# Where the output-projection steps stand in the opening half of a tile pair: behind each column part's down steps, or behind those of all parts

## The chip, the cores and the metric

The kernel runs on one core of one Trainium2 chip. Its engines here are PE (TensorE, the matrix engine; PEld are its weight loads), DVE (VectorE), ACT (ScalarE) and SP (SyncE, which issues DMAs). The metric is the device time of one execution in microseconds (us), the median of several runs.

## The reference

For 2048 tokens of width 640, the program computes a linear attention (32 heads of 20) and a feed-forward block (inner width 1728), and mixes them with a gate per token:

```
g = sigmoid((x * gate_w).sum(-1, keepdims=True))
a = attention(x) @ wo                                   # o: 2048 x 640, wo: 640 x 640
b = (gelu(x @ w_gate) * (x @ w_up)) @ w_down            # w_down: 1728 x 640
return g * a + (1 - g) * b
```

The two final products go to the same output. The kernel folds the gate ratio into the attention output, adds both products up in the same PSUM bank (a piece of the memory that matmuls write to), and scales once at the eviction.

## The kernel before

The change lies in the last stage. Tokens stand in 16 tiles of 128, taken in pairs; four tiles are a block. For each pair the output's 640 columns are cut into parts (320 + 320; in the last pair 256 + 256 + 128). For each part, the opening half of a pair takes 14 "down" steps (hidden chunk times `w_down`) and 5 "output-projection" steps (`goT`, the transposed and gated attention output, times `wo`). A step is two matmuls side by side, one on rows 0 to 63 of the array, one on rows 64 to 127. In the opening half of a pair, row half r works for tile r; in the closing half they swap, so that each tile gets both halves of the contraction.

```python
        # in down_pair(t0, banks, widths), a generator; mm() issues one matmul
        def mm(r, j, h, c, opens, x, n):          # row half r, tile j, part h, chunk c, step x of n
            ...
            w, end = widths[h], x == n - 1
            ...
            sc.op("pe", lambda e: e.matmul(self.bank(bk, w), lhs, rhs, start=opens and x == 0, stop=end and not opens,
                                           skip_group_check=True),
                  reads=rd, writes=[("ps", bk)] + ([("turn", bk)] if end else []), signal=end,
                  after=[("turn", bk)] if x == 0 and not opens else ())
        ...
        for q in range(2 * nw):
            h, opens = q % nw, q < nw
            cs = list(range(NFC + 1 if opens else NFC)) + [NFC + 1 + k for k in range(KD)]
            for x, c in enumerate(cs):
                for r in (0, 1):
                    mm(r, r if opens else 1 - r, h, c, opens, x, len(cs))
                if x == len(cs) - 1 and not opens:
                    evac(h)
                yield None
```

The closing half has 13 down steps, since the fourteenth chunk has only 64 rows and is done in one go. `after=[("turn", bk)]` is the wait at the swap: the first closing matmul into a bank waits until the other row half's last opening matmul into it has been written.

Between steps, the attention numerator of a later tile is computed (`num`): 20 short matmuls, a chain of VectorE operations that ends in the tile `Og`, and a DMA that transposes `Og` into `goT`. Positions are counted in steps of a block:

```python
        def downs(b, side):
            ...
                    n += 1
                    if n in side:
                        self.num(side[n])
        ...
        at = (1, 31, 61, 91)
        ...
        for b in range(self.NB):
            downs(b, {at[k]: 4 * b + 2 + k for k in range(4 if b < 3 else 2)})
```

In a block the second `num` makes `goT` for the fourth tile, which the second pair needs.

The softmax here doesn't subtract the row's maximum and nothing guards it: scores larger than these inputs give would overflow.

Of the kernel before, what the change touches and what calls it, by code (L numbers as in the profile page):

```python
# [107 lines left out]
class _Kernel:  # L108
    S, D, H, DH, F = 2048, 640, 32, 20, 1728
    KD = D // P  # L110
# [4 lines left out]
    NFC = 14  # L115
# [576 lines left out]
    def down_pair(self, t0, banks, widths):  # L692

        sc = self.sc
        ts = (t0, t0 + 1)
        NFC, KD = self.NFC - 1, self.KD
        nw = len(widths)
        hk = t0 // 4
        last = t0 + 2 == self.NT
        os_ = t0 % 4  # L700

        def mm(r, j, h, c, opens, x, n):
            t = ts[j]
            tt, gs, bk, w0, a = t % 4, t % 8, banks[h][j], sum(widths[:h]), 64 * r
            w, end = widths[h], x == n - 1
            if c <= NFC:
                lhs, rhs = self.hT(hk, c)[a:a + 64, tt * P:(tt + 1) * P], self.wd_sb[a:a + 64, c, w0:w0 + w]
                rd = [("hT", hk, c), "wd"] if c < NFC else [("hT", hk, 13, r), ("wd13", r)]
            else:
                k = c - NFC - 1  # L710
                lhs, rhs = self.goT[a:a + 64, gs, k, :], self.wo_sb[a:a + 64, k, w0:w0 + w]
                rd = [("goT", gs), "wo"]
# [5 lines that stand above are left out]
        def evac(h):  # L718
            w0, w = sum(widths[:h]), widths[h]
            for j in (0, 1):  # L720
                bk, dst, g = banks[h][j], self.outsb[:, os_ + j, w0:w0 + w], self.Gm[:, ts[j]:ts[j] + 1]
                rd, wr = [("ps", bk), "Gm"], [("outsb", os_ + j, h)]
                if last and j == 1:
                    sc.op("dve", lambda e: e.tensor_scalar(dst, self.bank(bk, w), g, None, op0=ALU.mult), reads=rd, writes=wr)
                else:
                    sc.op("act", lambda e: e.activation(dst, self.bank(bk, w), AF.Copy, scale=g), reads=rd, writes=wr)  # L726
            if last:
                hs, c0, c1 = [h], w0, w0 + w
            elif h == nw - 1:
                hs, c0, c1 = range(nw), 0, self.D  # L730
            else:
                return
            if t0 < self.TB:
                rows = self.out[0:self.BT, :].rearrange("(p j) n -> p j n", j=self.TB)[:, t0:t0 + 2, :]
            else:
                rows = self.out[t0 * P:(t0 + 2) * P, :].rearrange("(j p) n -> p j n", p=P)
            sc.dma("sp", lambda e: e.dma_start(rows[:, :, c0:c1], self.outsb[:, os_:os_ + 2, c0:c1]),
                   reads=[("outsb", os_ + j, k) for j in (0, 1) for k in hs], writes=[("out", t0, h)])

        for q in range(2 * nw):  # L740
            h, opens = q % nw, q < nw
            cs = list(range(NFC + 1 if opens else NFC)) + [NFC + 1 + k for k in range(KD)]
            for x, c in enumerate(cs):
                for r in (0, 1):
                    mm(r, r if opens else 1 - r, h, c, opens, x, len(cs))
                if x == len(cs) - 1 and not opens:
                    evac(h)
                yield None

# [94 lines left out]
```

## Time and profile before

| | before |
|---|---|
| time, median of 3 runs (range) | 288.31 us (287.94 to 288.32) |
| span of the profiled run | 287.0 us |
| last stage, from its first down matmul to the start of the last ScalarE eviction | 197.89 to 284.12 = 86.23 us |
| one step of 320 columns in it | 0.136 us |

The first view is the page: busy time of each engine, then two of the costliest groups. A group's columns are: source line, engine, operation, what is written and read, shape, count, then busy us and mean ns of one, then the engine's idle time just before.

```profile
PE 280.9 (98%) x3017; PEld 185.7 (65%) x3032; DVE 174.9 (61%) x353; ACT 104.5 (36%) x199; POOL 5.3 (2%) x36
...
L713 PE MATMUL ps<-wd_sb,hT 64*128 64x320 bf16 x648 | 49.4, 296 | 0.0
...
L713 PE MATMUL ps<-wo_sb,goT 64*128 64x320 bf16 (+2 forms) x340 | 27.8, 288 | 0.0
```

PE, the matrix engine, is busy 98% of the span. The 340 output-projection matmuls (those that read `goT`) and the 648 down matmuls shown had 0.0 us of idle time before them. They never waited for anything. The page's share of the chain that ended last says the same of the whole kernel:

```profile
PE 96%; DMA 2%; issue 1%; SPq 0%; ACT 0%
```

The chain in order of time (start us, length us, engine and line) shows the stage itself. L713 is the down and output-projection matmul, L657 the `num` matmul, L354 the matmuls of the stage before.

```profile
196.93 1.03 PE ps L354 x4
197.96 0.24 PE ps L713 x2
198.20 0.39 PE ps L657 x20
198.59 4.08 PE ps L713 x60
202.67 0.39 PE ps L657 x20
203.06 4.07 PE ps L713 x60
207.13 0.39 PE ps L657 x20
...
211.99 7.88 PE ps L713 x116
...
284.12 0.37 ACT outsb L726
```

The chain never leaves PE until the last eviction. A run of 60 matmuls is 30 steps in 4.07 to 4.08 us, 0.136 us each, and each `num` takes 0.39 us. The Trainium skill ("TensorE: Matmul & The Clock Gate", section Back-to-back issue gap) gives N/2.4 + 2.5 ns as the isolated warm gap, 135.8 ns for N = 320: this trace agrees. The stage is a sum of matmul times with nothing between them.

The timeline of ScalarE (start us, length us, operation, idle time before it and its end) gives the time at which banks come free; the first line is the end of the last pair but one, the second the end of the kernel's matmul work.

```profile
273.98 0.94 ACT L726 ACTIVATE outsb<-ps,Gm 128x320 bf16<-128x320 f32 x2 [1.50 <-PE ps L713]
...
284.12 0.37 ACT L726 ACTIVATE outsb<-ps,Gm 128x128 bf16<-128x128 f32 x1 [0.53 <-PE ps L713]
```

The two evictions of a part take 0.94 us together.

### The profile page before, as it was taken

Reading aid. Unit: us, or ns where it says so; the run is one execution under the profiler, and the core shown is the slowest. Engines: PE = TensorE matmul, PEld = TensorE weight load, DVE = VectorE, ACT = ScalarE, POOL = GpSimd, SP = SyncE. Lnnn points to the kernel's source line nnn. Section 1 sums busy time; section 2 is a strip of 40 time slices with the busy share of each in tenths; the row PEclk is TensorE's granted clock in tenths of the full one; section 3 lists DMA queues with packets and bytes.
Section 4 is the critical chain, followed back from the end, with each engine's and each line's share of the span. In section 5 each row is a group of like instructions: output and inputs, shape, how many; then the busy total and the mean of one; then the engine's idle time right before and its main releaser. Section 6 shows DMA issues by size and latency. Waiting matters only on the chain.

```text
span 287.0 us, 7005 instructions
## 1 busy us (share of the span) xinstructions
PE 280.9 (98%) x3017; PEld 185.7 (65%) x3032; DVE 174.9 (61%) x353; ACT 104.5 (36%) x199; POOL 5.3 (2%) x36
## 2 busy tenths in 40 slices
PE   7999999999999999999999999999999999999995
PEld 3576689999994444444444444445777777777785
DVE  1348999999977553567242334225883883883801
ACT  3357887677653222322323223321112112112111
POOL 7000000000000000000000000000000000000000
PEclk9999999999999999999999999999999999999999
DMA  8999996000002000011000000000232343342121
GB/s 224 203 174 248 366 366 192 0 2 2 2 0 48 0 0 0 3 24 23 2 0 0 0 2 0 0 2 0 26 87 74 29 48 99 43 60 82 49 72 48
DMA packets 36937, 18.67 MB, mean 65 GB/s; under 512 B 28970, under 2 KB 36394, under 8 KB 36906
## 3 DMA queue, kind: packets, MB, share of 16 engines
q1 hardware_dynamic: 36240, 18.19, 26.8%
q8 instruction: 24, 0.39, 0.6%
q10 hardware_dynamic: 666, 0.03, 0.2%
q14 instruction: 7, 0.06, 0.1%
HBM read 9.04 MB, written 2.62 MB: 41 GB/s over the span
## 4 chain that ended last, share of the span: by engine, by line
PE 96%; DMA 2%; issue 1%; SPq 0%; ACT 0%
PE ps L354 61%; PE ps L713 28%; PE ps L657 2%; PE ps L366 2%; PE ps L452 2%; DMA w<-in_A_wqkv_dram 2%; PE ps L334 1%; SPq L216 0%; ACT outsb L726 0%; PE ps L316 0%
## 5 line engine op out<-in xcount | busy, mean ns | idle before, releaser
L354 PE MATMUL ps<-xT,wg_sb 128*128 128x512 bf16 (+1 forms) x265 | 63.8, 379 | 0.4 <-issue 0.2
L354 PE MATMUL ps<-xT,wu_sb 128*128 128x512 bf16 (+1 forms) x263 | 63.3, 379 | 0.5 <-DVE hT L631 0.2
L629 ACT ACTIVATE gl<-ps 128x512 bf16<-128x512 f32 x52 | 30.9, 596 | 73.1 <-PE ps L354 68.7
L631 DVE TENSOR_TENSOR hT<-ps,gl 128x512 bf16<-128x512 f32 x39 | 26.7, 690 | 38.3 <-PE ps L354 38.2
L713 PE MATMUL ps<-wd_sb,hT 64*128 64x320 bf16 x648 | 49.4, 296 | 0.0
L354 PEld LDWEIGHTS ps<-xT,wu_sb 128*128 128x128 bf16 (+1 forms) x270 | 26.5, 99 | 29.7 <-DVE hT L631 0.5
L354 PEld LDWEIGHTS ps<-xT,wg_sb 128*128 128x128 bf16 (+1 forms) x270 | 26.2, 99 | 29.0 <-ACT gl L629 0.2
L354 PE MATMUL ps<-w,xT 128*64 128x512 bf16 (+6 forms) x398 | 41.6, 325 | 0.2
L726 ACT ACTIVATE outsb<-ps,Gm 128x320 bf16<-128x320 f32 (+2 forms) x31 | 14.5, 515 | 72.4 <-PE ps L713 72.4
L713 PEld LDWEIGHTS ps<-wd_sb,hT 64*128 64x128 bf16 x648 | 31.0, 94 | 12.2 <-issue 0.4
L354 PEld LDWEIGHTS ps<-w,xT 128*64 128x64 bf16 (+1 forms) x400 | 35.6, 107 | 5.0
L713 PE MATMUL ps<-wo_sb,goT 64*128 64x320 bf16 (+2 forms) x340 | 27.8, 288 | 0.0
L354 PE MATMUL ps<-xT,wq 128*64 128x512 bf16 (+1 forms) x184 | 25.9, 380 | 0.1
L436 DVE TENSOR_TENSOR Ek<-Ek,Dk 128x640 bf16<-128x640 bf16 x32 | 25.0, 822 | 0.6
L684 DVE TENSOR_TENSOR O<-ps,RH 128x640 bf16<-128x640 f32 x32 | 24.8, 816 | 0.0
L427 DVE TENSOR_REDUCE Dk<-Ek 128x64 f32<-128x1280 bf16 x16 | 23.7, 1479 | 0.0
L416 ACT ACTIVATE Ek<-ps 128x640 bf16<-128x640 f32 x32 | 20.7, 703 | 3.5 <-PE ps L354 3.5
L521 ACT ACTIVATE Eq<-ps 128x512 bf16<-128x512 f32 x40 | 21.6, 607 | 0.7 <-PE ps L354 0.4
L631 DVE TENSOR_TENSOR xT<-ps,gl 128x512 bf16<-128x512 f32 x13 | 9.0, 692 | 18.2 <-PE ps L354 18.2
L713 PEld LDWEIGHTS ps<-wo_sb,goT 64*128 64x128 bf16 x340 | 16.0, 94 | 5.4
L354 PEld LDWEIGHTS ps<-xT,wq 128*64 128x64 bf16 (+1 forms) x185 | 15.3, 108 | 2.9
L713 PE MATMUL ps<-wd_sb,xT 64*128 64x320 bf16 (+2 forms) x270 | 16.7, 269 | 0.0
(69 smaller groups left out, 172.9 us busy)
## 6 DMA issues: line engine op xcount, KB each, us to landing
out_dram<-outsb SPq DMA_DIRECT2D x7, 320.0 KB, 2.3
wd_sb<-in_B_w_down_dram SPq DMA_DIRECT2D x1, 2080.0 KB, 12.9
wg_sb<-in_B_w_gate_dram SPq DMA_DIRECT2D x1, 1120.0 KB, 5.8
wu_sb<-in_B_w_up_dram SPq DMA_DIRECT2D x1, 1120.0 KB, 9.5
wg_sb<-in_B_w_gate_dram SPq DMA_DIRECT2D x1, 960.0 KB, 9.6
wu_sb<-in_B_w_up_dram SPq DMA_DIRECT2D x1, 960.0 KB, 10.2
w<-in_A_wqkv_dram SPq DMA_DIRECT2D x5, 160.0 KB, 4.5
wo_sb<-in_A_wo_dram SPq DMA_DIRECT2D x1, 800.0 KB, 9.4
```

Of the source, the lines that this page charges most:

```text
L354: self.sc.op("pe", lambda e: e.matmul(self.ps[a:z, bank * 512 + c0:bank * 512 + c0 + n], lhs[:, a:z], rhs, start=first, stop=fin), reads=r ...
L366: sc.op("pe", lambda e, c0=c0, n=n, bk=bk, col=col: e.matmul(self.bank(bk)[:, col:col + n], self.xT[:, kt, t * P:(t + 1) * P], self.w3[:, ...
L416: self.sc.op("act", lambda e, s=s, scale=scale: e.activation(self.Ek[:, se, s, :], self.ps[:, o:o + self.D], AF.Exp, scale=scale), reads=[ ...
L427: sc.op("dve", lambda e: e.tensor_reduce(self.Dk[:, se, 0, :].rearrange("p (s h) -> p s h", h=H), self.Ek[:, se, :, :].rearrange("p s (h d ...
L436: sc.op("dve", lambda e, v=v, r=r: e.tensor_tensor(v, v, r, ALU.mult), reads=[("Rk", se)], writes=[("Ek", se, s)])
L452: sc.op("pe", lambda e: e.matmul(self.ps[a:a + 64, b * 512 + c:b * 512 + c + 2 * nf], va[:, lo:lo + 64], self.Ek[:, se, :, f0:f0 + nf], st ...
L521: sc.op("act", lambda e, s=s, scale=scale: e.activation(self.Eq[:, s, i, b * self.BT:(b + 1) * self.BT], self.bank(bank), AF.Exp, scale=sc ...
L629: sc.op("act", lambda e: e.activation(self.gl[:, slot, :], self.bank(banks[0]), AF.Gelu_apprx_tanh), reads=[("ps", banks[0])], writes=[("g ...
L631: sc.op("dve", lambda e: e.tensor_tensor(hT, self.bank(banks[1]), self.gl[:, slot, :], ALU.mult), reads=[("ps", banks[1]), ("gl", slot)], ...
L684: dve(lambda e, o=o, f=f, s=s: e.tensor_tensor(o, V[s][:, :, :, 0:DH], f, ALU.mult), rb + [key(6 + s)], [("O", s, sl)], guard=old)
L713: sc.op("pe", lambda e: e.matmul(self.bank(bk, w), lhs, rhs, start=opens and x == 0, stop=end and not opens, skip_group_check=True), reads ...
L726: sc.op("act", lambda e: e.activation(dst, self.bank(bk, w), AF.Copy, scale=g), reads=rd, writes=wr)
```

## The change

It puts the opening output-projection steps of all parts behind the opening down steps of all parts. The intent: `goT` is wanted 14 steps later (28 in the last pair), so a late `goT` would have more time to land.

```diff
-        for q in range(2 * nw):
-            h, opens = q % nw, q < nw
-            cs = list(range(NFC + 1 if opens else NFC)) + [NFC + 1 + k for k in range(KD)]
-            for x, c in enumerate(cs):
+        wos = [NFC + 1 + k for k in range(KD)]
+        opening = list(range(NFC + 1)) + wos
+        for part in (range(NFC + 1), range(NFC + 1, len(opening))):
+            for h in range(nw):
+                for x in part:
+                    for r in (0, 1):
+                        mm(r, r, h, opening[x], True, x, len(opening))
+                    yield None
+        closing = list(range(NFC)) + wos
+        for h in range(nw):
+            for x, c in enumerate(closing):
                 for r in (0, 1):
-                    mm(r, r if opens else 1 - r, h, c, opens, x, len(cs))
-                if x == len(cs) - 1 and not opens:
+                    mm(r, 1 - r, h, c, False, x, len(closing))
+                if c == closing[-1]:
                     evac(h)
                 yield None
```

## The prediction

> **What bounds the kernel now.** The page gives TensorE (PE) 98% busy at full granted clock, and the chain that ended last is 96% PE. The change touches only the last stage, 198.0 to 284.1 us. The chain in order of time is pure PE there: runs of 60 matmuls take 4.07 to 4.08 us, with 20 matmuls of a `num` step in 0.39 us between. Two matmuls (rows 0-63 and 64-127) run together, so one step takes 4.08/30 = 136 ns. The Trainium skill ("TensorE: Matmul & The Clock Gate", Back-to-back issue gap) gives N/2.4 + 2.5 ns warm, 135.8 ns for N = 320: the trace agrees, so the stage streams at its floor. Cross-check: 518 steps of 320 columns x 136 ns, 74 of 256 x 109, 37 of 128 x 56 and 14 `num` x 0.39 us make 86.0 us; the stage takes 86.1. There are no bubbles to remove. In the groups by line, idle before the output-projection matmuls (wo_sb, goT) is 0.0 us: they never wait for goT.
>
> **What the change does.** It adds and removes no instruction. The 10 output-projection matmuls of part 0 (0.68 us) move behind the 28 down matmuls of part 1. Three distances change:
> 1. goT is wanted 14 steps (1.9 us) later. Worth nothing, since nothing waits for it.
> 2. Part 1's banks are wanted after 14 steps, not 19: 1.9 us, not 2.6, after the preceding pair's last matmul. Their two evictions on ScalarE start 0.08 us after that matmul and take 0.94 us, so they are free after about 1.0 us. In the last pair steps have 256 columns: 14 x 0.109 = 1.53 us, still some 0.4 us ahead (estimate, less the early weight load).
> 3. Where the row halves swap banks ("turn"), the first closing matmul of part 0 waits for the last opening one of part 0. Between them stood 19 steps (2.6 us), now 5 (0.68 us). A matmul takes 0.30 us; the next is due about 0.82 us after its start; 0.1 us for the signal (as PE to ScalarE) and 0.1 for the early weight load leave about 0.3 us spare. No stall, but the tightest of the three.
>
> The `num` steps stay after steps 1, 31, 61, 91, so VectorE's 4.2 us per `num` meets the same 4.47 us period. The tail after the last matmul is unchanged.
>
> **On the critical path.** All of the stage is, but its length is a sum of matmul times, which a permutation leaves alone. Expected: 0.0 us (estimate); at worst 8 turns x about 0.1 us, if the signal is slower than taken.
>
> **Prediction.** 288.3 us, with 287.8 to 288.9 holding it 8 times in 10. Faster by over 2%: 0.5%; within 2%: 98.5%; slower by over 2%: 1%.
>
> **What would show it.** Right: the chain again has 4.08 us per 60 matmuls, the last stage 86.1 us within 0.2, idle before down and output-projection matmuls 0.0. Wrong at (3): a PE gap in every pair just after part 1's opening output-projection steps. Wrong at (2): a PE gap released by ScalarE's eviction, 14 steps into a pair. Wrong at (1), to the good: the stage shortens.
>
> **What would make it wrong.** A wait that stops PE's early weight loads well before its matmul is due would turn the 0.3 us spare into a stall of some tenths, up to 8 times: 1 to 2 us. Or VectorE's margin against `num` tips over: under 0.2 us each, 14 times.

## The result, and the profile after

The changed kernel took 288.22 us (median of 6 runs, 287.63 to 289.16) against 288.12 us for the kernel before (6 runs, 287.72 to 288.32). The ratio is 1.0007 with a 95% interval of 0.9986 to 1.0027: the same.

The page of the changed kernel, the same lines:

```profile
PE 281.0 (98%) x3017; PEld 185.6 (64%) x3032; DVE 174.8 (61%) x353; ACT 104.5 (36%) x199; POOL 5.3 (2%) x36
...
PE 93%; SPq 3%; DMA 2%; issue 1%; ACT 0%
...
L713 PE MATMUL ps<-wd_sb,hT 64*128 64x320 bf16 x648 | 48.5, 296 | 0.0
...
L713 PE MATMUL ps<-wo_sb,goT 64*128 64x320 bf16 (+2 forms) x340 | 26.5, 288 | 0.0
```

In the chain's shares the 3% of SPq, the queue that issues DMAs, belong to the start-up, which is looked at below. Idle time before both groups is again 0.0 us. The groups' busy time seems to fall, from 27.8 to 26.5 us for the output projection. That is no gain: a matmul's modelled length (296 ns) is more than twice the spacing of steps, so at each switch from one group to the other both count the same stretch, and the change has fewer switches. The timeline of PE shows it: where two runs of 10 output-projection matmuls stood apart, there is now one of 20.

```profile
214.24 1.52 PE L713 MATMUL ps<-wo_sb,goT 64*128 64x320 bf16 x20
```

The chain in order of time:

```profile
197.84 1.03 PE ps L354 x4
198.87 0.24 PE ps L713 x2
199.11 0.39 PE ps L657 x20
199.50 4.08 PE ps L713 x60
203.58 0.39 PE ps L657 x20
203.97 4.07 PE ps L713 x60
208.05 0.39 PE ps L657 x20
...
212.91 7.88 PE ps L713 x116
...
285.04 0.37 ACT outsb L726
```

It is the chain of before, piece for piece, 0.91 us later. From the first to the last line it is 86.17 us (285.04 less 198.87), and it was 86.16 (284.12 less 197.96). Measured from the first matmul's start on the timeline, the stage is 86.24 us against 86.23. The evictions keep their places too:

```profile
274.89 0.94 ACT L726 ACTIVATE outsb<-ps,Gm 128x320 bf16<-128x320 f32 x2 [1.50 <-PE ps L713]
...
285.04 0.37 ACT L726 ACTIVATE outsb<-ps,Gm 128x128 bf16<-128x128 f32 x1 [0.53 <-PE ps L713]
```

Where a wait comes close, the weight loads are held up before the matmuls are (by 0.15 us in e2_turn2 below, where seven of eight pairs lose nothing). In the stage of the changed kernel, the view of waits lists none of them as held up by PE, ScalarE or a DMA. Its only entry (engine, line, what was waited for, then us in total, times, longest), the same as in the kernel before:

```profile
PEld ps L713 <- issue: 0.4, 1, 0.4
```

So where do the 0.9 us come from by which the profiled span is longer (287.9 against 287.0 us)? Not from the stage. They are there when it begins. In the kernel before, the chain had early on one wait for a weight transfer, and in the changed kernel another one for the transposed input:

```profile
1.73 4.50 DMA w<-in_A_wqkv_dram
```

```profile
10.52 5.70 DMA xT<-in_A_x_dram
```

The lengths are those of the transfers; on the timeline PE itself sat idle for 1.11 us in the kernel before, and for 0.17 us (weights) and 1.74 us (input) in the changed one, which makes 0.80 of the 0.91 us. The change does not touch that part of the program, and PE's start-up wanders from run to run: in the profiles of kernels with a changed order the last stage begins anywhere between 197.77 and 198.92 us. All runs of the kernel before spread over 287.57 to 289.18 us, as wide as the 287.63 to 289.16 us of the changed one. Their spans do the same: 286.3 to 287.9 us in the 14 runs beside the experiments, 286.4 to 287.9 us in the six of the changed kernel, of which the profiled run was the slowest. That is why experiments are read below from the last stage of each profile, and why the whole time of a run only confirms it.

### The profile page after: what moved, and what is told of

Read it like the earlier page. It is cut to its first block, busy times and chain, and to the rows that moved or that the text cites. A ratio compares the mean times of both kernels' runs of the same rounds, so it can differ in the third digit from the quotient of the medians.

```text
span 287.9 us, 7005 instructions
## 1 busy us (share of the span) xinstructions
PE 281.0 (98%) x3017; PEld 185.6 (64%) x3032; DVE 174.8 (61%) x353; ACT 104.5 (36%) x199; POOL 5.3 (2%) x36
## 4 chain that ended last, share of the span: by engine, by line
PE 93%; SPq 3%; DMA 2%; issue 1%; ACT 0%
PE ps L354 60%; PE ps L713 28%; PE ps L657 2%; DMA xT<-in_A_x_dram 2%; PE ps L452 2%; SPq L220 1%; PE ps L334 1%; SPq L224 1%; SPq L239 1%; SPq L216 0%; ACT outsb L726 0%
## 5 line engine op out<-in xcount | busy, mean ns | idle before, releaser
L713 PE MATMUL ps<-wd_sb,hT 64*128 64x320 bf16 x648 | 48.5, 296 | 0.0
L354 PEld LDWEIGHTS ps<-xT,wu_sb 128*128 128x128 bf16 (+1 forms) x270 | 26.5, 99 | 29.7 <-DVE hT L631 0.5
L713 PE MATMUL ps<-wo_sb,goT 64*128 64x320 bf16 (+2 forms) x340 | 26.5, 288 | 0.0
L713 PE MATMUL ps<-wd_sb,xT 64*128 64x320 bf16 (+2 forms) x270 | 16.0, 269 | 0.0
```

Of the source, the lines that this page charges most:

```text
L354: self.sc.op("pe", lambda e: e.matmul(self.ps[a:z, bank * 512 + c0:bank * 512 + c0 + n], lhs[:, a:z], rhs, start=first, stop=fin), reads=r ...
```

## The experiments

The theory: the stage is a gapless sum of matmul times, so that order alone costs and gains nothing. An order matters only through three distances: from a `num` to the first step that needs its `goT`, from an eviction to the next use of its banks, and from the last opening matmul of a part to the first closing one (the turn). The change moves all three, and none of them binds in either kernel. A rival is that something else sets the pace, so that distances in the PE order don't matter; VectorE's `num` chain is the candidate: it takes some 4.2 us from its first operation to its last, of the 4.47 us between two `num` steps. A second rival is that a wait stops PE for a fixed time as soon as it is placed close. Each experiment makes one distance so small that the theory gives a number for it. Expectations quote the stage from the chain (86.1 to 86.2 us); the table measures it from the timeline, 0.07 us longer.

| run | stage us | against 86.23 | time us, median of 4 | ratio to before, 95% |
|---|---|---|---|---|
| before | 86.23 | | | |
| after | 86.24 | +0.01 | 288.22 (6 runs) | 1.0007 (0.9986 to 1.0027) |
| e1_turn0 | 88.35 | +2.12 | 289.98 | 1.0056 (1.0030 to 1.0082) |
| e2_turn2 | 86.38 | +0.15 | 288.24 | 1.0009 (0.9975 to 1.0043) |
| e3_bank1 | 92.88 | +6.65 | 294.67 | 1.0215 (1.0184 to 1.0245) |
| e3b_bank6 | 87.98 | +1.75 | 289.99 | 1.0061 (1.0036 to 1.0086) |
| e4_before_late | 95.39 | +9.16 | 297.59 | 1.0328 (1.0298 to 1.0357) |
| e5_after_late | 90.51 | +4.28 | 292.74 | 1.0150 (1.0124 to 1.0176) |
| e6_before_41 | 89.76 | +3.53 | 291.71 | 1.0120 (1.0097 to 1.0142) |
| e7_after_41 | 86.23 | 0.00 | 288.38 | 0.9999 (0.9969 to 1.0028) |

The kernel before, run beside them, had medians of 288.42 us (7 runs, with e1, e3, e4 and e5) and 287.98 us (7 runs, with the others). All results were correct.

### The turn: 0 steps and 2 steps of cover

The change leaves 5 steps between the last opening matmul of part 0 and the closing one that waits for it, where 19 stood. These two kernels leave none, and 2, by moving part 0's own output projection to the end of the opening half:

```diff
-        for part in (range(NFC + 1), range(NFC + 1, len(opening))):
-            for h in range(nw):
-                for x in part:
-                    ...
+        n1 = len(opening)
+        seq = [(h, x) for h in range(nw) for x in range(NFC + 1)]
+        behind = [(h, x) for h in range(1, nw) for x in range(NFC + 1, n1)]
+        cut = len(behind) - 0        # e2_turn2: - 2
+        seq += behind[:cut] + [(0, x) for x in range(NFC + 1, n1)] + behind[cut:]
+        for h, x in seq:
+            ...
```

> The change, but with the opening output-projection steps of part 0 put last, so that no step (instead of 5) stands between the last opening matmul of part 0 and the first closing one that waits for it. Theory (a turn costs only what its signal lacks in cover): the last opening matmul ends 0.30 us after its start, some 0.1 us for the signal and up to 0.1 us for the weight load bring the next start to 0.40 to 0.50 us instead of 0.136, so a PE gap of 0.27 to 0.37 us in each of 8 pairs: the last stage grows by 2.1 to 2.9 us, from 86.1 to 88.2 to 89.0 us. Rival A (a stopped queue must fill again, so a turn costs far more): gaps of 0.6 us or more, over 4.8 us in all. Rival B (PE keeps its order anyway and the wait is free): no gap, 86.1 us.

> As the run with no step between the halves' turn, but with 2 steps (output projection of part 1) between. With none the last stage measured 88.26 us, 2.2 more than 86.1, so 0.27 us per pair: the first closing matmul starts 0.41 us after the start of the matmul that it waits for. With 2 steps it is due after 3 x 0.136 = 0.41 us. Theory (only the cover counts): gaps of 0.0 to 0.05 us, stage 86.1 to 86.5 us; this puts the margin that the change leaves, with 5 steps, at 0.82 - 0.41 = 0.41 us. Rival (each turn placed close costs a fixed stop of PE's early loads): about 2 us again.

Measured: 2.12 us more without cover, and 0.15 us more with 2 steps. The timeline of the weight loads (PEld, which run just ahead of their matmuls) shows the wait at the first turn, of e1_turn0 and then of e2_turn2:

```profile
204.59 1.61 PEld L713 LDWEIGHTS ps<-wd_sb,hT 64*128 64x128 bf16 x26 [0.42 <-PE ps L713]
```

```profile
204.12 1.61 PEld L713 LDWEIGHTS ps<-wd_sb,hT 64*128 64x128 bf16 x26 [0.15 <-PE ps L713]
```

With no cover the load sits idle for 0.42 us before the turn, in every pair but the last (0.37 us); with two steps, for 0.15 us in each pair. The difference is two steps of 0.136 us, so the wait is neither free nor a fixed cost, and the rivals of these runs fall.

An idle load is not yet a lost matmul. Without cover the matmuls lose 2.12/8 = 0.265 us per pair, so the waiting matmul can start 0.136 + 0.265 = 0.40 us after the start of the one that it waits for. With two steps of 320 columns it is due after 3 x 0.136 = 0.41 us, and the seven pairs with such steps lose nothing: in e2_turn2 their pieces of the chain are the 4.08 and 7.88 us of before. All of the 0.15 us is lost in the last pair, where the two steps have 128 columns and take 0.056 us each. The last matmul piece of the chain, of the kernel before and then of e2_turn2:

```profile
268.07 16.03 PE ps L713 x308
```

```profile
268.36 16.18 PE ps L713 x308
```

There the matmul starts 0.109 + 2 x 0.056 + 0.15 = 0.37 us after the one that it waits for, and without cover 0.109 + 0.265 = 0.37 us. In the changed kernel it is due after 6 x 0.136 = 0.82 us (320 columns): the margin is about 0.4 us, and no time is lost.

### The banks: part 1 after 1 step and after 6

The change asks for part 1's banks 14 steps after a pair's beginning, not 19. These kernels cut the opening half after step 1 and after step 6, which leaves the turn its cover:

```diff
-        for part in (range(NFC + 1), range(NFC + 1, len(opening))):
+        for part in (range(1), range(1, len(opening))):     # e3b_bank6: 6 for both 1s
```

(Written as a list of steps, as above, with the same effect.)

> The change, but with the opening cut after step 1 and not after step 14: part 1's banks are wanted 1 step after the preceding pair's last matmul, while the turn keeps 18 steps. Theory (the distance to ScalarE's evictions matters once it is below about 1.1 us): the second eviction ends 1.02 us after the last matmul, signal and weight load add 0.1 to 0.2; due after 0.14 us at the 4 boundaries inside a block (gap about 1.0 us) and after 0.53 us at the 3 between blocks, where a num step stands in between (gap about 0.6 us), and about 0.3 us at the first: 6.1 us in all, the last stage 92 us (91 to 93), the time about 294.4 us. Rival (VectorE's num chain, 4.2 us of each 4.47 us, sets the pace, and PE order is hidden behind it): PE gaps are made up at the next num, and the stage grows by under 2 us.

> The opening cut after step 6. With the cut after step 1 the stage measured 92.8 us, 6.7 more: about 1.1 us at each boundary within a block, so part 1's second bank is usable about 1.36 us after the start of the preceding pair's last matmul. Cut after step 6 it is due after 0.95 us within a block (gap 0.4 us, 3 times), 0.79 us in the last pair with its 256 columns (gap 0.57), and 1.34 us between blocks (no gap). Theory: 1.8 us more, stage 87.6 to 88.2 us. With the change's own 14 steps it is due after 1.66 us in the last pair and 2.04 us elsewhere, so 0.3 us would be the smallest margin. Rival (a boundary costs a fixed amount however near): 6 us again, or a part of it that does not follow the distance.

Measured: 6.65 us more (6.1 expected), and 1.75 us more (1.8 expected). The weight loads at the first boundary inside a block, of e3_bank1 and of e3b_bank6:

```profile
210.88 0.09 PEld L713 LDWEIGHTS ps<-wd_sb,hT 64*128 64x128 bf16 x1 [0.82 <-ACT outsb L726]
211.30 1.74 PEld L713 LDWEIGHTS ps<-wd_sb,hT 64*128 64x128 bf16 x27 [0.32 <-ACT outsb L726]
```

```profile
209.82 0.09 PEld L713 LDWEIGHTS ps<-wd_sb,hT 64*128 64x128 bf16 x1 [0.17 <-ACT outsb L726]
210.24 1.33 PEld L713 LDWEIGHTS ps<-wd_sb,hT 64*128 64x128 bf16 x21 [0.33 <-ACT outsb L726]
```

The two row halves need two banks, which ScalarE frees one after the other; each half's load waits for its own eviction (0.82 and 0.32 us, then 0.17 and 0.33 us). The stage grows by what the distance lacks and by nothing else. It was not made up at the next `num`, so VectorE does not set the pace. The need worked out from the first of these runs, 1.36 us from the start of the preceding pair's last matmul, predicted the second to 0.05 us. The change's smallest distance is that of the last pair, 0.136 + 14 x 0.109 = 1.66 us, so the margin there is 0.3 us.

### The date of goT: late num steps, in both orders

Here the intent itself is tested: does the new order gain where `goT` is late? The second `num` of a block is moved from step 31 to 51, the third and fourth with it:

```diff
-        at = (1, 31, 61, 91)
+        at = (1, 51, 81, 111)     # in the kernel before (e4) and in the changed one (e5)
```

> The kernel before with the num steps after steps 1, 51, 81 and 111 of a block, not 1, 31, 61 and 91, so that the second num of a block stands 37 steps (5.4 us with the PE time of the next num) before the first output-projection step that needs it, not 57. Needed from a num's start on PE: 0.39 PE + 0.2 to VectorE + 4.2 VectorE + 2.6 transpose by DMA = 7.4 us. Theory (the change moves the date at which goT is wanted, which is worth something only where goT is late): PE waits for goT about 2.0 us in each of 4 blocks, 8 us in all, stage 94 us, time about 296 us. Rival (goT has more slack than this sum, or VectorE works faster apart from other num steps): no wait, 288 us.

> The changed kernel with the same late num steps (1, 51, 81, 111). The first output-projection step that needs the second num now comes 51 steps after it (7.3 us), against 7.4 us needed. Theory: PE waits 0.0 to 0.2 us in each of 4 blocks, under 1 us in all, so the stage is 86.1 to 87 us and the time 288.3 to 289.2 us: the change is worth about 7 us here, over 2%, where it was worth nothing in its own place. Rival (the order of the two kinds of steps makes no difference to PE's waits): the same time as the kernel before with late num steps.

Measured: 9.16 us more in the order before (8 expected; a fifth wait of 0.6 us for `goT`, in a first pair, was not), and 4.28 us more in the changed order, where I had expected under 1. The second expectation failed. The change does gain here, 4.9 us of stage, but it does not hide all of the delay. The PE timelines show the second `num` of the first block, the first output-projection matmul (its `goT` is there), and its neighbour on the other row half, which waits. First e4_before_late with the issue of the transpose from the queue of SyncE, then e5_after_late:

```profile
205.32 0.56 PE L657 MATMUL ps<-KV,Eq 64*128 64x88 bf16 x20
...
211.13 0.30 PE L713 MATMUL ps<-wo_sb,goT 64*128 64x320 bf16 x1
213.31 0.85 PE L713 MATMUL ps<-wo_sb,goT 64*128 64x320 bf16 x9 [1.89 <-DMA goT<-Og]
```

```profile
210.69 1.20 SPq L689 DMA_TRANSPOSE goT<-Og  x1
```

```profile
206.10 0.56 PE L657 MATMUL ps<-KV,Eq 64*128 64x88 bf16 x20
...
213.81 0.30 PE L713 MATMUL ps<-wo_sb,goT 64*128 64x320 bf16 x1
214.92 1.26 PE L713 MATMUL ps<-wo_sb,goT 64*128 64x320 bf16 x16 [0.82 <-DMA goT<-Og]
```

```profile
211.47 1.20 SPq L689 DMA_TRANSPOSE goT<-Og  x1
```

In e4 PE is 5.81 us past the start of the `num` when it wants `goT`, and waits until 7.99. In e5 it comes 7.71 us after the start and still waits until 8.82. My sum of 7.4 us was too small, in two terms. From the start of `num` to the issue of the transpose it took 5.37 us in both (0.39 + 0.2 + 4.2 = 4.8 in my sum); in later blocks of e5 5.1 us. And the transpose, which I had entered with its median of 2.6 us from issue to landing, has no fixed time: in the trace of e5 the four that PE waited for landed after 3.4, 4.0, 4.2 and 2.6 us. In e4 the transposes in the same places took 2.6 us each. The spread was there to be seen: the 14 transposes in the last stage of the kernel before landed after 2.6 to 4.3 us. (The number of steps is not to blame: I had counted 7.3 us of cover for e5, forgetting that two `num` stand in it; it was 7.7.)

The Trainium skill ("Perfetto Trace Analysis", section Per-instruction lifecycle) warns that for a DMA "the entire data movement" falls outside the profiled window, and this trace agrees: the transpose shows 1.20 us in its queue, and what waits for it waits for 3.4 us from the same start.

With this corrected need, 7.7 to 9.7 us, step 41 was chosen, where the order before should fall short and the changed one hardly:

```diff
-        at = (1, 31, 61, 91)
+        at = (1, 41, 71, 101)     # in the kernel before (e6) and in the changed one (e7)
```

> The kernel before with num steps after steps 1, 41, 71, 101. From a num's start on PE to the issue of its transpose took 5.1 to 5.4 us in the runs with 51, and the transpose 2.6 to 4.3 us to land: 7.7 to 9.7 us. Here PE reaches the step that needs it 47 steps and 2 num (7.2 us) after its start. Theory: PE waits 0.5 to 2.4 us for goT in each of 4 blocks, 2 to 8 us in all, so stage 88 to 94 us and time 290.5 to 296 us. Rival (the late num cost time by VectorE's order, not by goT's date): no wait for goT.

> The changed kernel with num steps after steps 1, 41, 71, 101. PE now reaches the step that needs goT 61 steps and 2 num (9.1 us) after the num's start, against 7.7 to 9.7 us needed. Theory: waits of 0 to 0.6 us, under 1.5 us in all, stage 86.1 to 87.6 us, time 288.3 to 289.9 us: the order of the change hides here what the order before does not. Rival: the same time as the order before with these num steps.

Measured: 3.53 us more in the order before, and 0.00 us in the changed order. Two of e6's waits were not expected: in the first pairs of the last two blocks the weight loads sat idle for 0.34 and 0.50 us, for transposes that took 4.2 and 4.4 us. The group of the output projection in the stage, for e6_before_41 and then e7_after_41:

```profile
L713 PE MATMUL ps<-wo_sb,goT 64*128 64x320 bf16 (+2 forms) x340 | 32.7, 289 | 2.3 <-DMA goT<-Og 2.2
```

```profile
L713 PE MATMUL ps<-wo_sb,goT 64*128 64x320 bf16 (+2 forms) x340 | 26.3, 288 | 0.0
```

PE waits for `goT` in the one and never in the other. That e7 lost nothing at all had luck in it: the four transposes in question landed after 2.6 us each, another in the same trace after 4.4 us. With that one the sum would be 5.0 + 4.4 = 9.4 us against 9.1 us of cover, a wait of some 0.3 us (an estimate). The two ratios to the kernel before, 1.0120 and 0.9999, have intervals that don't touch. So the mechanism that the change aims at is real, and 3.5 us large here (1.2%). In the kernel as it stands, with `num` at step 31, it has nothing to remove.

That was close, though. In the kernel before, the last pair's `goT` was issued at 272.55 us and landed 2.6 us later, at 275.15, and the first matmul that reads it started at 275.27:

```profile
272.55 1.20 SPq L689 DMA_TRANSPOSE goT<-Og  x1
```

```profile
275.27 0.71 PE L713 MATMUL ps<-wo_sb,goT 64*128 64x256 bf16 x10
```

In the other blocks the same distance is 0.5 to 0.9 us. These four transposes all took 2.6 us; one of 4.3 us, as another in that trace, would have made PE wait. So the change removes no wait that was there, but it widens the thinnest margin of the stage by 14 steps (28 in the last pair). Whether a late transpose ever costs the kernel before time is not shown: the one execution of it that is traced has none.

None of the experiments points to a kernel that beats both. Every one has the gapless stage at best, and e7 shows that the freedom won (a later `num`) buys no time by itself. A faster stage would need less matmul work, not another order.

## Why the prediction was right

It said 288.3 us (287.8 to 288.9) and the same time; measured were 288.22 us and a ratio of 1.0007. Point by point:

- "The stage streams at its floor", "no bubbles to remove": right. The chain of the changed kernel repeats that of before piece for piece, 4.07 to 4.08 us for 60 matmuls.
- goT wanted later is "worth nothing, since nothing waits for it": right, shown from both sides. Idle time is 0.0 us in both kernels, and with `num` ten steps later the same change of order is worth 3.5 us. How near `goT` already came, 0.1 us in the last pair, the prediction did not say.
- The banks, "some 0.4 us ahead" in the last pair: right that it doesn't bind; the margin worked out from e3_bank1 and borne out by e3b_bank6 is 0.3 us.
- The turn, "about 0.3 us spare", "the tightest of the three": it doesn't bind; its margin is 0.4 us, so the banks of the last pair are tighter. The sum took the matmul's end, a signal and the weight load one after another (0.5 us); measured were 0.40 us. The two margins were thus off by 0.1 us, one each way, and their ranking was wrong; neither decided the result.
- VectorE "meets the same 4.47 us period": right, the `num` steps keep their places in the chain. That PE and not VectorE sets the pace is shown by e3_bank1, where lost PE time is not made up.

The step that did go wrong came later, in the expectation for e5_after_late: the time from a `num` to its `goT` was summed with a median (2.6 us) for a transfer that took up to 4.4 us in these traces. What decides whether a transpose takes 2.6 or over 4 us was not tested and stays open. The output store that follows does not by itself: it was issued 1.37 us after the first of these transposes in both e4 and e5, and the transposes took 2.6 and 3.4 us.

## What to carry to other kernels

Before reordering work on the bounding engine, look whether it ever idles before the instructions that you want to move: with 0.0 us there, and steps at their streaming time, a permutation has nothing to gain and can only move margins. Idle time of 0.0 us does not say how wide they are: here one was 0.1 us. Work out each distance that the new order shortens and compare it with what its wait needs; then squeeze that distance on purpose, for the size of the wait shows how much room was left. For a date that depends on a DMA, take the slowest landing in the trace and not the median.

## What the Trainium skill lacked or had wrong

- "TensorE: Matmul & The Clock Gate", section Back-to-back issue gap, gives a sustained 131 ns per matmul at N = 512 in a stream of loads and matmuls, and calls N/2.4 + 2.5 ns (216 ns) an over-count there. In this kernel 42 such matmuls (128 x 512, each with its own weight load) took 9.06 us in a row, 216 ns each, by this piece of the chain of the kernel before:

```profile
187.81 9.06 PE ps L354 x42
```

- The same section gives 81 ns sustained at N = 128. With two row halves side by side, the 128-column steps of the last pair took 56 ns for two matmuls (28 matmuls from 277.89 to 278.68 us in the kernel before).
- The same page, Part 3, The mechanism, says that matmuls start and end in program order. After one row half had waited (e5_after_late), the records show the other ahead of it: an output-projection matmul, which stands behind all 20 `num` matmuls in the program, starts 0.02 us before one of the last of them. The timeline of PE there, cut to 0.04 us:

```profile
216.22 0.37 PE L657 MATMUL ps<-KV,Eq 64*128 64x88 bf16 x10
216.41 0.30 PE L713 MATMUL ps<-wo_sb,goT 64*128 64x320 bf16 x1
216.43 0.20 PE L657 MATMUL ps<-KV,Eq 64*128 64x88 bf16 x1
```

- "DMA: Bandwidth & Descriptors", section Anatomy of one DMA, fits 2.0 us + bytes / 436 GB/s for DMAs issued from GpSimd, and I found no time from issue to landing for a transpose of this size issued from SyncE (there are bandwidths for transposes, and a time for a tile of 128 x 128). By that fit a tile of 128 x 640 two-byte elements would take 2.4 us (an estimate from the page). Here such a transpose landed 2.5 to 4.5 us after its issue in the last stages of the ten traces; the spread is what the page lacks.
- No page that I read says how close a wait of PE on PE's own earlier matmul may stand without loss. Here 0.40 us from start to start, about three steps of 320 columns (0.37 us in the last pair, with 256).
